# Sixteen instead of eight weight pairs of a second FFN layer by seven block products, with the small elementwise steps placed anew

## The chip, the cores and the metric

The kernel runs on one core of one Trainium2 chip. The metric is the time of one execution on the device in microseconds (us). The engines have short names in the profile: PE is the matrix engine (TensorE), PEld its weight loads, DVE is VectorE, ACT is ScalarE, POOL is GpSimd, and SP (SyncE) issues nearly all DMAs.

## The reference, cut to what matters

```python
xn = _layernorm(x)                                  # x: 2048 x 576
# attention: 32 heads of 18, eight dilated positions (0, 2, .. 14 back) for each token
qkv = xn @ wqkv                                     # 576 x 1728
o = attend(qkv) @ wo                                # 576 x 576
# feed-forward, beside the attention
h = xn @ w1 + b1                                    # 576 x 4608
act = h * tanh(softplus(h))                         # Mish
out = x + o + act @ w2                              # 4608 x 576
```

All values are 32-bit floats. Each matrix product is made of three: both factors are split into a rounded high part and the rest (the low part), and high x high, high x low and low x high are summed in PSUM. Every operand of a product therefore costs elementwise work: a copy to the rounded type on ACT (high) and a subtraction on DVE or POOL (low).

## The kernel before, in words

The 2048 tokens are worked on in two halves of 1024, each split into two blocks b of 512. The hidden width 4608 is cut into 18 pairs q of two 128-wide tiles (j = 0, 1). In each half the plan runs through the QKV products, and then through 18 **quads**, one for a pair q: six parts of the first FFN layer (`m1_part`, L715, already by seven block products) with the second FFN layer's work for the pair before (`add` and `quad`, L1140 to L1270) between them. The second half takes the pairs in the order 1 to 17, then 0 (`Q1`, L33). A last stage multiplies the attention by `wo` (`wo_part`, L1038).

The second FFN layer exists in two forms. In the plain form (`m2_pair` L748, `m2_cols` L861) a quad has four chunks, each of 24 matmuls of 128 x 288 and four DVE additions from PSUM into an accumulator. In the form by **seven products** (`p_item`, L835), which the second half uses for the first `2 * OC` pairs, two pairs are taken together (index e): with the token blocks as rows, the two hidden tiles as the inner index and the two 288-wide column halves as columns, a 2 x 2 block product takes seven products P1 to P7 in place of eight. An item is one product for two pairs: again 24 matmuls of 128 x 288 and four evictions. Two plain quads have 8 chunks, two quads by seven products have 7 items.

For this the left factors S1 to S4 are sums and differences of the activations (`u_sum` L782), and they and the unchanged blocks are split by `u_high` (L792) and `u_low` (L797). The right factors are blocks B11, B21, B22 of w2 and their differences T1 to T4. These are made in half one, when w2 is loaded anyway: `t_sum` (L293), `t_high` (L305), `t_low` (L310), `t_keep` (L315); `keep` (L260) stores the blocks. They go to DRAM and `p_fetch` (L812) brings them back. At the end of that form `p_join` (L855) adds the accumulators of P1, P6 and P7 into those of P2 to P5. One more pair (`a_split`, L804) holds its raw activations and goes the plain way.

Beside this, attention runs as a generator of steps on POOL (products), DVE (reductions) and ACT (exponentials) (`attention`, L512). Its steps are handed to plan slots by weights (`marks`, `rate`, L1481 to L1501). The same 7-product form is used for part of QKV (`z_...`, L383 to L408) and for `wo`; their weight differences are made in half one from quad 9 on (`z_...`, L1376 to L1386) and in half two from quad 11 on (`wo_keep_...`, L1503 to L1514).

The order of instructions on every engine is the order in which the program emits them: for each plan slot first what was put there by `before` (L1144), then the slot's matmuls (L1533 to L1537). Nothing is reordered at run time, so an instruction that waits holds up all behind it on its engine. The lines that place what the change touches:

```python
def before(i, fn):
    plan[max(i, 0)][1].append(fn)
...
for q in range(1, 2 * OC + 1):
    i = spot(0, q, (3,2)[q > 1])
    for (f, name), d in zip(((t_sum, "T3"), (t_sum, "T1"), ...
...
seven = lambda hf, q: hf == 1 and q <= 2 * OC
```

Of the kernel before, what the change touches and what calls it, by code (L numbers as in the profile page):

```python
# [31 lines left out]
OC = 4  # L32
# [5 lines left out]

@with_exitstack
def block_kernel(ctx: ExitStack, tc: tile.TileContext, x, wq, wo, w1, b1, w2, mask, out):  # L40
    nc = tc.nc
    tpn = iter(range(1000))

# [50 lines left out]
    XNB = 5  # L94
# [149 lines left out]
    def make(kind, i):  # L244
        load({"wa": "w1", "wc": "w1", "t0": "w1", "t1": "w1"}.get(kind, kind), i)
        width = home(kind, i)[2]
        if kind == "wa":
            src = loaded["w1", i][0]
        elif kind == "wc":
            src = loaded["w1", i][1][:, 2 * P:5 * P]  # L250
        elif kind in ("t0", "t1"):
            src = sums[i][int(kind[1])]
        else:
            src = loaded[kind, i][:, 0:width]
        t = done[kind, 0, i] = new(kind, 0, i)
        nc.scalar.copy(t[:, 0, :], src)
        low[kind, i] = lambda: nc.vector.tensor_tensor(out=t[:, 1, :], in0=src, in1=t[:, 0, :].bitcast(F32),
                                                       op=ALU.subtract)
# [34 lines left out]
    def t_sum(q, name):  # L293
        eng = nc.vector if name in ("T3",) else nc.gpsimd
        if name in ("T3", "T2"):
            tw[q, name] = sb.tile([P, 5 * P], F32, tag="xn", bufs=XNB, name=f"tw{name}_{q}")[:, 0:D].rearrange(
                "p (c d) -> p c d", c=2)
# [12 lines left out]
    def t_low(q, name):  # L310
        eng = nc.vector
# [60 lines left out]
    zkept, zw, zq, zraw, zhi = {}, {}, {}, {}, {}  # L372
# [10 lines left out]
    def z_load(name, k):  # L383
        t = zraw[name, k] = sb.tile([P, 5 * P], F32, tag="xn", bufs=XNB, name=f"z{name}_{k}")[:, 0:432]
        i = z_unit(name, k)
        nc.sync.dma_start(t, wq[i // 5, i % 5])

    def z_sum(name, k):
        x, y = ZT[name]
        out_ = {"T1": "B12", "T2": "B22", "T4": "B21"}.get(name)  # L390
        if out_ is None:
            zraw[name, k] = sb.tile([P, 5 * P], F32, tag="xn", bufs=XNB, name=f"z{name}_{k}")[:, 0:432]
        else:
            zraw[name, k] = zraw[out_, k]
        nc.gpsimd.tensor_tensor(out=zraw[name, k], in0=zraw[x, k], in1=zraw[y, k], op=ALU.subtract)

    def z_high(name, k):
        hi = zhi[name, k] = sb.tile([P, 5 * P], F32R, tag="xn", bufs=XNB, name=f"zh{name}_{k}")[:, 0:432]
        nc.scalar.copy(hi, zraw[name, k])

    def z_low(name, k):
        t, hi = zraw[name, k], zhi[name, k]
        nc.vector.tensor_tensor(out=t.bitcast(F32R), in0=t, in1=hi.bitcast(F32), op=ALU.subtract)

    def z_keep(name, k):
        d = zkept[name, k] = dram.tile([P, 2 * 432], F32, name=f"kept_{name}_{k}")
        nc.sync.dma_start(d[:, 0:432], zhi[name, k].bitcast(F32))
        nc.sync.dma_start(d[:, 432:864], zraw[name, k])  # L408
# [101 lines left out]
    pend, soon = [], []  # L510

    def attention(hf):  # L512
# [9 lines left out]
        for pair in range(NQ * UQ // PU):  # L522
# [34 lines left out]
            if (hf, pair) == (0, 4):  # L557
                soon.append(lambda: nc.scalar.preload_act_table_set("natural_log_exp_and_others"))
            soon.append(lambda Ls=Ls: nc.scalar.activation(Ls, Ls, AF.Exp, scale=SCALE))
            if (hf, pair) == (0, 4):  # L560
                soon.append(root1)
# [80 lines left out]
    def s_low(hf, c, k):  # L642
        t, hi, lo = stmp[hf, c, k]
        nc.vector.tensor_tensor(out=lo, in0=t, in1=hi.bitcast(F32), op=ALU.subtract)
# [48 lines left out]
    def mish(hf, q, b, j, ph, t=None):  # L693
# [6 lines left out]
        def run():  # L700
# [8 lines left out]
            nc.gpsimd.tensor_tensor(out=a[:, 1, :], in0=t, in1=a[:, 0, :].bitcast(F32), op=ALU.subtract)  # L709
        if q or b != j:  # L710
            pend.append(run)
        else:
            late.append(run)
# [53 lines left out]
    def rslotof(q, x):  # L767
        k = q, int(x[1]) - 1, int(x[2]) - 1
        assert owner[where[k]] == k, (k, owner[where[k]])
# [12 lines left out]
    def u_sum(e, k, qq):  # L782
        name, q = LEFT[ORD[k]], 2 * e + qq
        eng = nc.gpsimd if (name, qq) in (("S1", 1), ("S4", 0)) else nc.vector
# [12 lines left out]
    def u_low(e, k, qq):  # L797
        name, q = LEFT[ORD[k]], 2 * e + qq
        u = unit(e, k, qq)
        eng = nc.gpsimd if (name, qq) in (("S3", 0), ("A22", 0), ("A22", 1), ("A11", 0), ("A11", 1), ("S1", 0), ("A12", 0), ("S2", 0)) else nc.vector  # L800
        eng.tensor_tensor(out=u[:, 1, :], in0=u_src(q, name),  # L801
                          in1=u[:, 0, :].bitcast(F32), op=ALU.subtract)

    def a_split(b, j):  # L804
        q = 2 * OC
        t = rawact[q, b, j]
        assert owner[where[q, b, j]] == (q, b, j) and (q, f"A{b + 1}{j + 1}") in held_
# [47 lines left out]
    def p_join(a, b, pr):  # L855
        nc.gpsimd.tensor_tensor(out=pacc[a, pr], in0=pacc[a, pr], in1=pacc[b, pr], op=ALU.add)  # L856
# [80 lines left out]
    ops, wo_t, wraw, traw = {}, {}, {}, {}  # L937

    wkept, whi = {}, {}

    def wo_keep_high(name, n):
        if name in ("R", "D"):
            src = wraw["R"][:, 0:D] if name == "R" else wraw["D"]
        else:
            src = wo_src(name).rearrange("p k c -> p (k c)")
        w = HC if name == "D" else D
        tag = ("r3", "xn")[n % 2]
        h = sb.tile([P, 2 * 432] if tag == "r3" else [P, 5 * P], F32R, tag=tag, bufs=(1, XNB)[n % 2], name=f"woh_{name}")[:, 0:w]
        whi[name] = h, src
        nc.scalar.copy(h, src)  # L950
        if name == "R":
            d = wraw["D"] = sb.tile([P, 4 * P], F32, tag="tt", bufs=2, name="wo_d")[:, 0:HC]
            nc.gpsimd.tensor_tensor(out=d, in0=src[:, 0:HC], in1=src[:, HC:D], op=ALU.subtract)

    def wo_keep_low(name):
        h, src = whi[name]
        nc.vector.tensor_tensor(out=src.bitcast(F32R), in0=src, in1=h.bitcast(F32), op=ALU.subtract)

    def wo_keep(name):
        h, src = whi[name]  # L960
        w = HC if name == "D" else D
        d = wkept[name] = dram.tile([P, 2, w], F32, name=f"wkept_{name}")
        nc.sync.dma_start(d[:, 0], h.bitcast(F32))
        nc.sync.dma_start(d[:, 1], src)
# [20 lines left out]

    def wo_load(k):
        name = ("B12", "B11", "B21", "B22")[k]
        k0, c0 = (int(name[1]) - 1) * 2 * P, (int(name[2]) - 1) * HC
        wraw[name] = sb.tile([P, 5 * P], F32, tag="raw", bufs=4, name=f"r{name}")[:, 0:D].rearrange(
            "p (k c) -> p k c", k=2)  # L990
        nc.sync.dma_start(wraw[name], wo[k0:k0 + 2 * P, c0:c0 + HC].rearrange("(k p) c -> p k c", p=P))

    def wo_sum(n):
        if n == 0:
            for name in ("T3", "T1", "T2", "T4"):
                traw[name] = sb.tile([P, 5 * P], F32, tag="xn", bufs=XNB, name=f"raw_{name}")[:, 0:D].rearrange(
                    "p (k c) -> p k c", k=2)
        name, x, y = (("T3", "B22", "B12"), ("T1", "B12", "B11"), ("T2", "B22", "T1"), ("T4", "B21", "T2"))[n]
        nc.gpsimd.tensor_tensor(out=traw[name], in0=wo_src(x), in1=wo_src(y), op=ALU.subtract)

    def wo_src(name):
        return (traw if name[0] == "T" else wraw)[name]

    def wo_high(name):
        nc.scalar.copy(wo_t[name][:, 0], wo_src(name))

    def wo_low(name):
        eng = nc.gpsimd if name in ('B21', 'T4') else nc.vector
        eng.tensor_tensor(out=wo_t[name][:, 1], in0=wo_src(name), in1=wo_t[name][:, 0].bitcast(F32),
                                op=ALU.subtract)  # L1010

    def wo_rest(step):
        if step == 0:
            wraw["R"] = raw_load(wo[4 * P:5 * P, :], D, "wo_r")
            return
        r = wraw["R"][:, 0:D].rearrange("p (c d) -> p c d", c=2)
        if step == 1:
            nc.scalar.copy(wo_t["R"][:, 0], r)
            nc.vector.tensor_tensor(out=wo_t["R"][:, 1], in0=r, in1=wo_t["R"][:, 0].bitcast(F32), op=ALU.subtract)
            d = wraw["d"] = sb.tile([P, HC], F32, tag="mn", bufs=5, name="wo_d")  # L1020
            nc.gpsimd.tensor_tensor(out=d, in0=r[:, 0], in1=r[:, 1], op=ALU.subtract)
        else:
            d = wraw["d"]
            nc.scalar.copy(wo_t["D"][:, 0], d)
            nc.vector.tensor_tensor(out=wo_t["D"][:, 1], in0=d, in1=wo_t["D"][:, 0].bitcast(F32), op=ALU.subtract)
# [114 lines left out]
    def add(tag, *fns, alias=None):  # L1140
        at[tag] = at[alias] = len(plan)
        plan.append((list(fns), [], PART[tag[3]] if tag[0] == "m" else US[tag[0]]))

    def before(i, fn):  # L1144
        plan[max(i, 0)][1].append(fn)
# [171 lines left out]

    def bring(kind, i, slot, lead, lag=0):
        before(slot - lead, lambda: load(kind, i))
        before(slot, lambda: make(kind, i))  # L1320
        before(slot + lag, lambda: low[kind, i]())
        before(slot + lag + 3, lambda: keep(kind, i))
# [53 lines left out]
    i = spot(0, 9, 4)  # L1376
    for k in range(2):
        for n, steps in enumerate((
# [205 lines left out]
```

## Time and profile before

| what | value |
| --- | --- |
| median of three runs | 1123.52 us (1123.42 to 1124.13) |
| span of the profiled execution | 1121.6 us |
| instructions in it | 18415 |
| granted TensorE clock, mean of the core | 1.000 |
| PE / PEld busy | 1109.5 / 1023.0 us |
| DVE / POOL / ACT busy | 829.0 / 787.7 / 492.1 us |
| DMA | 271.08 MB, 242 GB/s on average |

The page of the profile tells of one profiled execution from its first to its last instruction; no time of its own stands beside its span. The three runs are timed around the whole execution, and their median is 1.9 us above the span. "Busy" counts instructions from start to end, and for DVE and POOL this takes in what an instruction waits after it has started. The views used below are: the page itself, the list of waits (who waited for whom), the timeline (instructions in order of time, neighbours of one kind merged), busy time by stretches, and groups of instructions by line and shape.

### The profile page before, as it was taken

The numbers are of one execution on the slowest core, as the hardware profiler recorded it, in microseconds if no ns is written. First come the engines' busy times: TensorE is split into PE (matmuls) and PEld (weight loads), VectorE is DVE, ScalarE is ACT, GpSimd is POOL, SyncE is SP. The second block draws the span as 40 slices with busy tenths as digits, with TensorE's granted clock in tenths as the row PEclk, the third lists the DMA queues.
The fourth block names the chain that finished last, engine by engine and source line by source line (L and its number), as shares of the span: only waits on it lengthen the run. The fifth ranks groups of instructions, "written<-read, shape, count | busy, mean of one in ns | idle before, by whom it ended". The sixth has DMA issues, their size and how long they took to land.

```text
span 1121.6 us, 18415 instructions
## 1 busy us (share of the span) xinstructions
PE 1109.5 (99%) x6630; PEld 1023.0 (91%) x6630; DVE 829.0 (74%) x1351; ACT 492.1 (44%) x892; POOL 787.7 (70%) x639
## 2 busy tenths in 40 slices
PE   8999999999999999999999999999999999999998
PEld 7999899999999999899999889999999999999998
DVE  6368788888888888877655456687866677776876
ACT  5544645544554545455233355343433343443332
POOL 2488767767689687676788476665789878668632
PEclk9999999999999999999999999999999999999999
DMA  6899885868767849666596797655655477676463
GB/s 200 283 312 318 290 283 205 289 228 284 261 240 258 282 163 345 222 240 214 191 342 238 231 373 249 241 200 174 227 198 189 168 263 269 215 253 248 157 222 104
DMA packets 147487, 271.08 MB, mean 242 GB/s; under 512 B 30114, under 2 KB 86724, under 8 KB 147396
## 3 DMA queue, kind: packets, MB, share of 16 engines
q1 hardware_dynamic: 147396, 269.91, 69.2%
q8 instruction: 52, 0.85, 0.3%
q14 instruction: 39, 0.32, 0.1%
HBM read 160.39 MB, written 109.48 MB: 241 GB/s over the span
## 4 chain that ended last, share of the span: by engine, by line
PE 89%; DVE 4%; POOL 3%; DMA 2%; issue 1%; ACT 1%; DVEq 0%; POOLq 0%; SPq 0%
PE h L657 28%; PE po L755 19%; PE pq L349 11%; PE po L868 10%; PE po L847 7%; PE h L663 5%; PE o L1056 4%; PE z L447 2%; DMA acc<-in_x 1%; POOL accP L856 1%; DVE u L801 1%; POOL pr L534 0%; DVE accP L871 0%; POOL act L709 0%; DMA z_B<-kept_wq 0%
## 5 line engine op out<-in xcount | busy, mean ns | idle before, releaser
L755 PEld LDWEIGHTS po<-w,act 128*128 128x128 f32 x1728 | 236.4, 188 | 7.5 <-DVE acc L759 1.7
L755 PE MATMUL po<-w,act 128*128 128x288 f32 x1728 | 240.8, 295 | 1.4 <-DVE acc L759 1.2
L534 POOL TENSOR_TENSOR pr<-q,kv 128x576 f32<-128x576 f32 x128 | 195.7, 1553 | 18.7 <-DMA q<-q_d 16.9
L572 POOL TENSOR_TENSOR pv<-L,kv 128x576 f32<-128x576 f32 x128 | 174.3, 1461 | 38.7 <-DVE L L565 20.9
L709 POOL TENSOR_TENSOR act<-c,act 128x512 fp32r<-128x512 f32 x81 | 107.1, 1322 | 128.4 <-ACT act L708 125.5
L759 DVE TENSOR_TENSOR acc<-po,acc 128x288 f32<-128x288 f32 x288 | 120.4, 450 | 31.6 <-PE po L755 30.2
L349 PE MATMUL pq<-wq,xt 128*128 128x432 f32 x672 | 136.2, 361 | 1.8 <-ACT xt L83 1.8
L868 PEld LDWEIGHTS po<-w,act 128*128 128x128 f32 x960 | 131.1, 188 | 3.7 <-DVE accP L871 0.4
L868 PE MATMUL po<-w,act 128*128 128x288 f32 x960 | 133.8, 295 | 0.2
L349 PEld LDWEIGHTS pq<-wq,xt 128*128 128x128 f32 x672 | 125.0, 188 | 8.7 <-ACT xt L83 2.7
L703 ACT ACTIVATE c<-c,b1c 128x512 f32<-128x512 f32 x81 | 58.7, 724 | 132.9 <-DVE c L702 132.6
L657 PE MATMUL h<-xt,t 128*128 128x512 f32 x432 | 110.6, 391 | 0.9 <-DVE c L702 0.8
L657 PE MATMUL h<-S,t 128*128 128x512 f32 x432 | 110.4, 391 | 0.0
L691 ACT COPY c<-h 128x512 f32<-128x512 f32 x81 | 47.4, 586 | 136.5 <-PE h L663 78.3
L578 DVE TENSOR_REDUCE og<-pv 128x144 f32<-128x1152 f32 x64 | 85.9, 1343 | 25.4 <-POOL pv L572 25.4
L657 PE MATMUL h<-xt,wa 128*128 128x512 f32 x432 | 104.0, 390 | 0.0
L657 PEld LDWEIGHTS h<-xt,wa 128*128 128x128 f32 x432 | 80.9, 188 | 16.9
L871 DVE TENSOR_TENSOR accP<-po,accP 128x288 f32<-128x288 f32 x160 | 69.6, 454 | 36.1 <-PE po L868 34.5
L847 PEld LDWEIGHTS po<-pw,u 128*128 128x128 f32 x672 | 92.4, 188 | 2.9 <-DVE u L801 0.5
L847 PE MATMUL po<-pw,u 128*128 128x288 f32 x672 | 94.2, 296 | 0.3 <-DVE u L801 0.3
L539 DVE TENSOR_REDUCE L<-pr 128x64 f32<-128x1152 f32 x64 | 85.8, 1341 | 11.2 <-POOL pr L534 11.1
L657 PEld LDWEIGHTS h<-xt,t 128*128 128x128 f32 x432 | 79.0, 188 | 16.1 <-DVE c L702 1.1
(231 smaller groups left out, 1840.5 us busy)
## 6 DMA issues: line engine op xcount, KB each, us to landing
kv<-kv_d SPq DMA_DIRECT2D x64, 396.0 KB, 5.2
kept_t<-t SPq DMA_DIRECT2D x36, 512.0 KB, 5.3
t<-kept_t SPq DMA_DIRECT2D x36, 512.0 KB, 5.4
rw<-in_w SPq DMA_DIRECT2D x36, 320.0 KB, 4.6
kept_wa<-wa SPq DMA_DIRECT2D x18, 640.0 KB, 3.5
kept_w<-w SPq DMA_DIRECT2D x20, 576.0 KB, 4.8
wa<-kept_wa SPq DMA_DIRECT2D x18, 640.0 KB, 6.1
w<-kept_w SPq DMA_DIRECT2D x20, 576.0 KB, 4.5
```

Of the source, the lines that this page charges most:

```text
L349: nc.tensor.matmul(pq[:, 0:432], XT[:, xi, tok], wt[wi][:, hl, 0:432], start=i == 0, stop=i == len(seq) - 1)
L534: nc.gpsimd.tensor_tensor(out=pr[:, x:x + hh], in0=q[:, j0 + x:j0 + x + hh, None, :].to_broadcast([P, hh, W, CU]), in1=win(kt, 0, CU, j0 + ...
L539: nc.vector.tensor_reduce(L[:, k, j0:j0 + hj].rearrange("p j w h -> p (j w h)"), pr.rearrange("p j w (h d) -> p (j w h) d", h=2), axis=AX, ...
L572: nc.gpsimd.tensor_tensor(out=pr[:, x:x + hj].rearrange("p j d w -> p j w d"), in0=L[:, k, x:x + hj, :, h:h + 1].to_broadcast([P, hj, W, DH]),
L578: nc.vector.tensor_reduce(og[:, :, c0:c0 + DH], pr, axis=AX, op=ALU.add)
L657: nc.tensor.matmul(ph, wt[:, wl, wk * P:(wk + 1) * P], X[:, xs, :], start=first and i == 0, stop=last and i == len(seq) - 1, skip_group_ch ...
L709: nc.gpsimd.tensor_tensor(out=a[:, 1, :], in0=t, in1=a[:, 0, :].bitcast(F32), op=ALU.subtract)
L755: nc.tensor.matmul(po, acts[hf, q, b, j][:, al, tok], done["w2", hf, 2 * q + j][:, wl, c * HC:(c + 1) * HC], start=i == 0, stop=i == 5)
L759: nc.vector.tensor_tensor(out=t, in0=po, in1=t, op=ALU.add)
L847: nc.tensor.matmul(po, units[e, k, qq][:, al, tok], w[:, qq, wl, :], start=i == 0, stop=i == 5)
L868: nc.tensor.matmul(po, acts[hf, q, b, j][:, al, tok], done["w2", hf, 2 * q + j][:, wl, c * HC:(c + 1) * HC], start=i == 0, stop=i == 5)
L871: nc.vector.tensor_tensor(out=t, in0=po, in1=t, op=ALU.add)
```

## The change

- `OC` goes from 4 to 8, so that pairs 1 to 16 (and not 1 to 8) go by seven products in half two. The pair after them, held raw and split by `a_split`, is now the one before the last. The differences of w2 and the block-wise storing follow for pairs 9 to 16.
- The lists `pend` and `soon` and the slots' lists give way to one timeline with six positions for a plan slot. Each elementwise step, load, store and attention step has a key. A table `MOVE` of some 1,600 keys shifts the step by a number of positions (most by less than 20, some by up to 66), and two lists name steps that go to DVE or to POOL instead of their old engine.
- The low half of an activation (`run_low`) is placed apart from the Mish and the high half (`run`).
- The differences and splits of QKV and `wo` weights share one set of functions (`d_load` to `d_keep`), all placed in half one from quad 2 on. `wo`'s leave half two.
- The pool `xn` has 6 buffers instead of 5; T3 and T2 of w2 take buffers of `acc` and `r3`.
- The attention's rates change: 0.6 instead of 0.5 for quads 1 to 8 of half one, and 0.6 instead of 0.8 for quads 9 to 16; in half two 1.0 from quad 2 to quad 16, where 0.8 stood to quad 9 and 1.5 after it.

```diff
-OC = 4
+OC = 8
...
+MOVE = {"0 s_high": -6, "0 s_low": 18, "0 s_step": 3, ... }
+ON_VECTOR = ("act 0_0_12", "act 0_0_13", ... )
+ON_GPSIMD = ("d_low 0 T1", "d_low 1 T1", ... )
...
+    def engine(default, *key):
+        k = " ".join(str(x) for x in key)
+        return nc.vector if k in ON_VECTOR else nc.gpsimd if k in ON_GPSIMD else default
...
-    XNB = 5
+    XNB = 6
...
+    def put(pos, fn, key):
+        pos += MOVE.get(key, 0)
+        assert pos > now[0], key
+        timeline[pos].append(fn)
...
-            nc.gpsimd.tensor_tensor(out=a[:, 1, :], in0=t, in1=a[:, 0, :].bitcast(F32), op=ALU.subtract)
+
+        def run_low():
+            if not seven(hf, q):
+                a = acts[hf, q, b, j]
+                engine(nc.gpsimd, "act", n).tensor_tensor(out=a[:, 1, :], in0=t, in1=a[:, 0, :].bitcast(F32), op=ALU.subtract)
         if q or b != j:
-            pend.append(run)
+            soon(1, 3, run, "mish", n)
+            soon(1, 3, run_low, "act", n)
...
-    def before(i, fn):
-        plan[max(i, 0)][1].append(fn)
+    def before(i, fn, key=None, phase=1):
+        put(max(i, 0) * U + phase, fn, key or name_of(fn))
...
+    i = spot(0, 2, 5)
+    for m, lists in ((0, DIFFS), (1, DIFFS), ("w", DIFFS), ("w", SPLITS)):
...
-             spot(1, 2, 0), spot(1, 2 * OC + 2, 0), spot(1, NP - 1, 0), at["o", 0, 0], at["o", 2, 0]]
-    rate = (1.15, 0.4, 0.5, 0.8, 1.15, 1.3, 1.2, 0.8, 1.5, 0.8, 0)
+             spot(1, 2, 0), spot(1, NP - 1, 0), at["o", 0, 0], at["o", 2, 0]]
+    rate = (1.15, 0.4, 0.6, 0.8, 1.15, 1.3, 1.2, 1.0, 0.8, 0)
```

Counted in the lists, with the keys that no step has left out. To DVE: 29 activation lows of half one (and one of half two), 22 differences of w2, 9 differences of QKV and `wo` weights, 27 `u_low`, 5 `u_sum`, 3 joins. To POOL: 25 lows of loaded weights, 14 `t_low`, 6 lows of QKV and `wo` differences, 4 `s_low`, 17 `u_low`, 18 `u_sum`.

More of the change, by code (lines that the diff above doesn't have):

```diff
@@ L256, in make @@
         nc.scalar.copy(t[:, 0, :], src)
-        low[kind, i] = lambda: nc.vector.tensor_tensor(out=t[:, 1, :], in0=src, in1=t[:, 0, :].bitcast(F32),
+        low[kind, i] = lambda: engine(nc.vector, "low", kind, i).tensor_tensor(out=t[:, 1, :], in0=src, in1=t[:, 0, :].bitcast(F32),
                                                        op=ALU.subtract)
@@ L310, in t_low @@
     def t_low(q, name):
-        eng = nc.vector
+        eng = engine(nc.vector, "t_low", name, q)
         t = tw[q, name]
@@ L397, in z_high @@
[L397 to L408, printed above, removed]
+    PLACE = {"T1": "B11", "T3": "B12", "T2": "B22", "T4": "B21"}
@@ new lines, in d_sum, with d_high @@
+    def d_sum(m, name):
+        if name == "D":
+            r = zraw[m, "R"]
+            x, y, o = r[:, 0:HC], r[:, HC:D], d_tile(m, name)
+        else:
+            x, y = (zraw[m, n] for n in ZT[name])
+            o = zraw[m, PLACE[name]]
+        zraw[m, name] = o
+        engine(nc.gpsimd, "d_sum", m, name).tensor_tensor(out=o, in0=x, in1=y, op=ALU.subtract)
+    def d_high(m, name):
+        hi = zhi[m, name] = d_tile(m, name + "h", F32R)[:, 0:zraw[m, name].shape[1]]
+        nc.scalar.copy(hi, zraw[m, name])
@@ new lines, in d_low, with d_keep @@
+    def d_low(m, name):
+        t, hi = zraw[m, name], zhi[m, name]
+        engine(nc.vector, "d_low", m, name).tensor_tensor(out=t.bitcast(F32R), in0=t, in1=hi.bitcast(F32), op=ALU.subtract)
+    def d_keep(m, name):
+        w = zraw[m, name].shape[1]
+        if m == "w":
+            d = wkept[name] = dram.tile([P, 2, w], F32, name=f"wkept_{name}")
+            nc.sync.dma_start(d[:, 0], zhi[m, name].bitcast(F32))
+            nc.sync.dma_start(d[:, 1], zraw[m, name])
+        else:
+            d = zkept[name, m] = dram.tile([P, 2 * 432], F32, name=f"kept_{name}_{m}")
+            nc.sync.dma_start(d[:, 0:432], zhi[m, name].bitcast(F32))
+            nc.sync.dma_start(d[:, 432:864], zraw[m, name])
@@ L508, in win, with soon, name_of @@
                        ap=[list(base.ap[0]), [CU, jn], [DIL * CU, W], [1, cn]])
-    pend, soon = [], []
+    U = 6
+    now = [0]
+    timeline = []
+    def put(pos, fn, key):
+        pos += MOVE.get(key, 0)
+        assert pos > now[0], key
+        timeline[pos].append(fn)
+    def soon(slots, phase, fn, *key):
+        i = now[0] // U + slots
+        if phase == 3 and i == at["m", 0, 1, 0]:
+            phase = 5
+        put(i * U + phase, fn, " ".join(str(x) for x in key))
+    def name_of(fn):
+        text = lambda x: x.__name__ if callable(x) else str(x)
+        d = [text(x) for x in fn.__defaults__ or ()]
+        return " ".join([x for x in fn.__code__.co_freevars if x not in ("kind", "i", "at", "JB")][:1] + d)
     def attention(hf):
@@ L643, in s_low @@
         t, hi, lo = stmp[hf, c, k]
-        nc.vector.tensor_tensor(out=lo, in0=t, in1=hi.bitcast(F32), op=ALU.subtract)
+        engine(nc.vector, "s_low", hf, c, k).tensor_tensor(out=lo, in0=t, in1=hi.bitcast(F32), op=ALU.subtract)
     acts = {}
@@ L984, in wo_home @@
             wo_t["D"] = t[:, 3, :, 0]
[L986 to L1025, printed above, removed]
     ys = {}
@@ L1315, in block_kernel @@
             add(("o", p, part), lambda p=p, part=part: wo_part(p, part))
+    timeline.extend([] for _ in range((len(plan) + 3) * U))
+    now[0] = -1
+    for i, (fns, _) in enumerate(plan):
+        timeline[i * U + 4].extend(fns)
     def bring(kind, i, slot, lead, lag=0):
[L1319 to L1322, printed above, removed]
+        before(slot - lead, lambda: load(kind, i), f"load {kind} {i}")
+        before(slot, lambda: make(kind, i), f"make {kind} {i}")
+        before(slot + lag, lambda: low[kind, i](), f"low {kind} {i}")
+        before(slot + lag + 3, lambda: keep(kind, i), f"keep {kind} {i}")
     for k in range(5):
@@ L1429, in block_kernel @@
         for c in range(2):
-            before(at["q", 0, 3, 0, 0], lambda c=c, f=f: f(0, c, 3))
+            before(at["q", 0, 3, 0, 0], lambda c=c, f=f: f(0, c, 3), f"{f.__name__} first {c} 3")
     i = at["q", 1, 0, 1, 1]
@@ L1531, in block_kernel @@
             before(at["o", k // 2 - 1, 1], lambda k=k: y_load(k))
-    for i, (fns, bg, _) in enumerate(plan):
-        first, soon[:] = soon[:], []
-        held, pend[:] = pend[:], []
-        for fn in first + bg + (fns + held if i == at["m", 0, 1, 0] else held + fns):
+    for pos, fns in enumerate(timeline):
+        now[0] = pos
+        for fn in fns:
             fn()
```

117 lines of the change are left out of this document (45 added, 72 removed), and 4 rows, old and new, of the table i.

## The prediction

> **What bounds the kernel now.** I read the page first, then who makes PE wait, then PE's timeline around the quads.
>
> ```profile
> span 1121.6 us, 18415 instructions
> PE 1109.5 (99%) x6630; PEld 1023.0 (91%) x6630; DVE 829.0 (74%) x1351; ACT 492.1 (44%) x892; POOL 787.7 (70%) x639
> PEclk9999999999999999999999999999999999999999
> ```
>
> PE is busy in 1109.5 of 1121.6 us, at the full granted clock in all slices. 12.1 us of idle PE are all that better placing alone could win, and part of that is start and end.
>
> ```profile
> ...
> PE o L1056 <- DVE y L1060: 1.3, 2, 0.7
> PE po L755 <- DVE acc L759: 1.2, 1, 1.2
> ...
> PE h L657 <- DVE c L702: 0.8, 1, 0.8
> PE h L657 <- ACT rt L691: 0.7, 1, 0.7
> PE po L847 <- DVE u L801: 0.3, 1, 0.3
> ```
>
> Columns: sum, times, longest. These are the waits of PE behind the start: 4.3 us in six places, 0.72 us each. So time goes only where PE gets less work or new waits. The timeline gives the price of a quad; the rows are the first matmuls of `m1_part` in every second quad, three times by seven products, then twice in the plain form.
>
> ```profile
> 698.54 2.88 PE L657 MATMUL h<-xt,wa 128*128 128x512 f32 x12
> ...
> 743.76 2.88 PE L657 MATMUL h<-xt,wa 128*128 128x512 f32 x12
> ...
> 789.49 2.88 PE L657 MATMUL h<-xt,wa 128*128 128x512 f32 x12
> ...
> 920.27 2.89 PE L657 MATMUL h<-xt,wa 128*128 128x512 f32 x12
> ...
> 968.53 2.89 PE L657 MATMUL h<-xt,wa 128*128 128x512 f32 x12
> ```
>
> Two plain quads take 968.53 - 920.27 = 48.26 us. Two quads by seven products take 45.22 and 45.73 us. The kernel has both forms beside each other, so the main term can be read off directly.
>
> **The change, part by part.**
>
> *Matmuls (removed).* OC from 4 to 8 turns eight more quads, four couples e, into the second form. By the two stretches a couple saves 48.26 - 45.22 = 3.04 or 48.26 - 45.73 = 2.53 us, 2.79 in the mean. The chain of waits gives the same from single pieces:
>
> ```profile
> 703.24 3.24 PE po L847 x24
> ...
> 910.38 3.18 PE po L868 x24
> ```
>
> 8 x 3.18 - 7 x 3.24 = 2.76 us. Four couples: 4 x 2.79 = 11.1 us, between 10.1 and 12.2. I take 11.1, since it holds the small stalls that the form shows already.
>
> *Elementwise work of half two (added).* Groups by line and shape; the last numbers of a row before the second bar are busy us and mean ns.
>
> ```profile
> L709 POOL TENSOR_TENSOR act<-c,act 128x512 fp32r<-128x512 f32 x81 | 107.1, 1322 | 128.4 <-ACT act L708 125.5 <-DMA kv<-kv_d 2.2 <-DMA rw<-in_w 0.8
> L871 DVE TENSOR_TENSOR accP<-po,accP 128x288 f32<-128x288 f32 x160 | 69.6, 454 | 36.1 <-PE po L868 34.5 <-POOL accP L856 0.5 <-issue 0.3
> L853 DVE TENSOR_TENSOR accP<-po,accP 128x288 f32<-128x288 f32 x100 | 40.6, 448 | 7.2 <-PE po L847 6.6 <-POOL accP L833 0.2
> L801 POOL TENSOR_TENSOR u<-ra,u 128x512 fp32r<-128x512 f32 x14 | 18.9, 1354 | 4.7 <-ACT u L795 4.5
> L801 DVE TENSOR_TENSOR u<-rm,u 128x512 fp32r<-128x512 f32 x12 | 11.8, 981 | 3.6 <-ACT u L795 3.6
> L789 POOL TENSOR_TENSOR ra<-ra,rm 128x512 f32<-128x512 f32 x4 | 6.3, 1578 | 0.2
> L789 DVE TENSOR_TENSOR rm<-rt,rm 128x512 f32<-128x512 f32 x6 | 6.1, 1046 | 0.0
> L795 ACT CAST u<-ra 128x512 fp32r<-128x512 f32 x22 | 13.5, 619 | 17.1 <-DVE ra L789 8.4 <-PE po L847 6.9 <-POOL ra L789 1.8
> ```
>
> A couple gains 14 `u_low` (8 x 1.354 on POOL, 6 x 0.981 on DVE) and 8 sums (2 x 1.578, 6 x 1.046), loses 8 activation lows (8 x 1.322), and evicts 28 x 0.448 in place of 32 x 0.454: 10.8 + 5.9 + 3.2 + 6.3 - 10.6 - 2.0 = 13.6 us on DVE and POOL together, 54 for four. ACT gets 6 more copies a couple and 16 in half one, 40 x 0.62 = 25 us on 492: no bound.
>
> *Weight differences (added and moved to half one).*
>
> ```profile
> L303 POOL TENSOR_TENSOR twT<-rw,twT 128x288 f32<-128x288 f32 x16 | 15.9, 997 | 1.3
> L313 DVE TENSOR_TENSOR twT<-twT,twhT 128x576 fp32r<-128x576 f32 x16 | 13.8, 894 | 0.3
> L303 POOL TENSOR_TENSOR twT<-rw 128x288 f32<-128x288 f32 x8 | 9.9, 1235 | 0.0
> L303 DVE TENSOR_TENSOR twT<-rw,rw 128x288 f32<-128x288 f32 x8 | 9.8, 1223 | 0.0
> L957 DVE TENSOR_TENSOR raw_T<-raw_T,woh_T 128x576 fp32r<-128x576 f32 x4 | 5.0, 1238 | 0.0
> L257 DVE TENSOR_TENSOR w<-rw,w 128x576 fp32r<-128x576 f32 x36 | 44.1, 1228 | 5.3 <-ACT w L256 5.3
> ```
>
> Each of eight more quads gets 1.223 + 1.235 + 2 x 0.997 + 2 x 0.894 = 6.2 us, 50 in all. `wo`'s 14 subtractions come over from half two, about 14 x 1.24 = 17 us.
>
> *Does PE cover it?* Busy time by stretches (columns: length, then PE, PEld, DVE, ACT, POOL, clock, DMA share, GB/s):
>
> ```profile
> 145.00:532.00 387.00, 385.75 (x2352) 353.82 (x2351) 326.89 (x521) 194.71 (x317) 284.61 (x240) 1.00 0.71 251
> 338.00:435.00 97.00, 97.00 (x590) 88.93 (x589) 83.28 (x124) 46.17 (x76) 79.93 (x61) 1.00 0.72 256
> 655.00:837.00 182.00, 181.57 (x1090) 165.46 (x1089) 134.96 (x210) 80.12 (x135) 126.40 (x91) 1.00 0.67 233
> 837.00:862.00 25.00, 25.00 (x155) 22.97 (x154) 13.63 (x25) 6.16 (x10) 25.00 (x20) 1.00 0.47 170
> 862.00:1007.00 145.00, 145.00 (x879) 132.79 (x878) 105.47 (x170) 58.20 (x87) 110.11 (x84) 1.00 0.66 229
> 1007.00:1058.00 51.00, 50.57 (x334) 47.31 (x332) 38.91 (x69) 17.58 (x28) 41.07 (x33) 1.00 0.64 227
> ```
>
> Half two (655 to 1058): DVE 293 + POOL 303 = 596 of 806 engine-us, 74%. After: 596 + 54 - 17 = 633 of 2 x 392, 81%. Half one (145 to 532): 327 + 285 = 612 of 774, 79%; after: 612 + 50 + 17 = 679, 88%; attention's rates leave its total there about as it is (8 x 0.5 + 8 x 0.8 against 16 x 0.6, on weights that sum to less). The row 338 to 435 has (83.28 + 79.93) of 194, 84%, with PE busy in 97.00 of 97.00. So half two stays inside what PE is seen to cover, half one goes 4 points beyond.
>
> *Engine changes.* In half one DVE gets 29 activation lows (0.981) and 31 differences (1.223), gives 22 weight lows (1.228; three more lie ahead of the stretch), 14 `t_low` (0.894), 6 lows (1.238). With 8 x (1.223 + 2 x 0.894) and 9 of `wo` x 1.238 this is 326.9 + 24.1 + 11.1 + 28.4 + 37.9 - 27.0 - 12.5 - 7.4 = 381.5 of 387 us, 99%; POOL comes to some 303, 78%. But these durations hold waiting:
>
> ```profile
> 245.19 1.29 POOL L709 TENSOR_TENSOR act<-c,act 128x512 fp32r<-128x512 f32 x1
> ...
> 245.46 1.63 DVE L257 TENSOR_TENSOR w<-rw,w 128x576 fp32r<-128x576 f32 x1
> ...
> 261.82 0.76 DVE L257 TENSOR_TENSOR w<-rw,w 128x576 fp32r<-128x576 f32 x1
> ```
>
> The same DVE subtraction takes 0.76 us or, begun under a POOL instruction, 1.63: it ends at 247.09, 0.61 us behind POOL's end at 246.48. With 0.76/1.228 on all that DVE gains (101.5 us) its need is 343 us, 89%. I take the middle, 94%: full, but with deadlines that the slots' lead can meet. In-order queues make the cost: behind a subtraction that waits stand the evictions, and behind these PE, which needs free PSUM.
>
> *Removed waits.* The 4.3 us of PE waits may partly go with the new places, or others come: between -4.3 and, in half one, the rival below. I take 0.
>
> *Stores and fetches.* Eight quads of half one store 7 x 288 KB instead of 2 x 576, by the program: 864 KB more in 24.2 us, 36 GB/s on 256, a DMA share of about 0.82 after 0.72. A store waits on SP for its low half, with the loads of later quads behind it:
>
> ```profile
> SPq L275 <- DVE w L257: 48.9, 14, 6.2
> ```
>
> The longest such wait, 6.2 us, is a quarter of a quad, and loads go out five slots (about half a quad) ahead. Nothing at this cover; without it a late load would stop PE for some us in a quad. In half two four couples fetch 28 blocks of 576 KB where eight plain quads fetched 16: 12 more transfers in some 180 us at a share of 0.66, hidden.
>
> *Joins.* They move from 820 to 866 us to the last quad and the chunks behind it: no change but for the rival below.
>
> *Sum.* 1121.6 - 11.1 = 1110.5 us of span. The runs' median is 1.9 us above the span: **1112.4 us**.
>
> **The rivals.**
>
> *DVE late in half one.* For it: 89 to 99% of DVE. Against it: the row at 84% of both engines shows no wait at all. A wait of 0.72 us in every second of 16 quads is 5.8 us: 1118 us.
>
> *Slower: DVE and POOL read SBUF by turns.* For it: the rows at 245 and 261 us. Count all POOL time as holding and each DVE subtraction with its 0.76: now, in 338 to 435, 79.9 + (24 weight lows + 8 of QKV) x 0.76 = 104 of 97 us, 1.07, and PE doesn't wait. So the count is too high by at least that. After the change half one has about 303 + 179 x 0.76 = 439 of 387, 1.13 (74 weight lows, 29 activation lows, 31 differences, 16 T3, 18 `t_low`, 11 others). If 1.07 were the ceiling, half one would need 439/1.07 = 410 us: 23 us more than now, 1135 us. It decides from 1.07 on. Against it: many are 288 to 512 wide and shorter than 0.76, and moving a low from POOL (1.322) to DVE shortens the sum. The Trainium skill's page "SBUF — State Buffer", section "Who interferes with whom", says that a DVE instruction with two SBUF inputs and a POOL instruction that reads SBUF exclude each other for the whole instruction, so that moving work between the two frees less than it seems. By that rule the two rows agree (0.61 us behind POOL's end), and the time would be this rival's.
>
> *The last quads.*
>
> ```profile
> L856 POOL TENSOR_TENSOR accP<-accP,accP 128x576 f32<-128x576 f32 x14 | 20.5, 1485 | 1.2 <-DVE accP L853 1.2
> ```
>
> 11 of 14 joins stay on POOL, 11 x 1.485 = 16.3 us in a stretch where it has 41.07 of 51: 57 of 51 if no attention leaves it. At most 6 us late: 1118.
>
> *Placing also wins.* All six waits go and the couples reach 3.04: 1123.5 - 12.2 - 4.3 = 1107 us.
>
> That the change does not do what it says is excluded by the count of items that the program asserts (L1401).
>
> **How the numbers follow.** Forecast (1109 to 1115) 0.62; DVE late (1115 to 1122) 0.17; by turns 0.07; last quads 0.07; placing wins 0.07. I call 0.2% (2.2 us) what a measurement can tell: faster is below 1121.3, slower above 1125.8. Faster: 0.62 + 0.15 + 0.07 + 0.07 = 0.91, less 0.01 for what I don't see: 0.90. Same 0.04 (the end of DVE late and the beginning of by turns), slower 0.06. The range 1108.5 to 1120 leaves out about 0.04 below and 0.10 above.
>
> **What would show it.** Right: quads 9 to 15 of half two at 45.2 to 45.7 us a couple, PE busy near 1098 us, L868 with 8 x 96 = 768 fewer matmuls and L847 with 672 more, quads of half one still 24.1 us apart. Wrong: half one's quads further apart with PE waiting for DVE's evictions (L759) or additions (L702), DVE subtractions well above 1.2 us in the mean, or PE waiting at the end for accumulators that POOL joins.

## The result and the profile after

| | before | after |
| --- | --- | --- |
| median, four runs each on one chip | 1123.47 us | 1108.51 us (1107.54 to 1110.24) |
| ratio, 95% interval | | 0.9868 (0.9854 to 0.9882) |
| span of the profiled execution | 1121.6 us | 1106.9 us |

The change gains 15.0 us where 11.1 were forecast (1112.4 us, range 1108.5 to 1120). Of its four executions, two had a mean granted clock of 0.998 and spans of 1106.9 and 1107.6 us, two 1.000 and 1106.4 and 1105.8; the profile is of the first. The page of the changed kernel:

```profile
span 1106.9 us, 18216 instructions
PE 1097.6 (99%) x6534; PEld 1012.0 (91%) x6534; DVE 864.5 (78%) x1419; ACT 509.6 (46%) x933; POOL 818.3 (74%) x659
```

96 matmuls are gone. PE's busy time falls by 11.9 us and its idle time by 2.8 (12.1 to 9.3): together the 14.7 us of the span. Who makes PE wait (sum, times, longest), all there is:

```profile
PE z L477 <- DVE zqs L490: 1.8, 1, 1.8
PE warm L76 <- POOL ident masks.py:199: 1.3, 1, 1.3
PE pq L359 <- ACT xt L92: 1.2, 2, 0.6
PE h L705 <- ACT rt L739: 0.7, 1, 0.7
PE o L1041 <- DVE y L1045: 0.6, 1, 0.6
PE pq L359 <- POOL wq L1158: 0.2, 1, 0.2
```

The waits for the second FFN layer (`po`) and for `c` are gone; one in the z stage (QKV of half two by seven products, between the halves) is new. The couples of half two in the timeline, every second quad:

```profile
698.72 2.88 PE L705 MATMUL h<-xt,wa 128*128 128x512 f32 x12
...
743.75 2.93 PE L705 MATMUL h<-xt,wa 128*128 128x512 f32 x12
...
788.82 2.93 PE L705 MATMUL h<-xt,wa 128*128 128x512 f32 x12
...
834.29 2.93 PE L705 MATMUL h<-xt,wa 128*128 128x512 f32 x12
...
879.36 2.93 PE L705 MATMUL h<-xt,wa 128*128 128x512 f32 x12
...
924.44 2.93 PE L705 MATMUL h<-xt,wa 128*128 128x512 f32 x12
...
969.68 2.93 PE L705 MATMUL h<-xt,wa 128*128 128x512 f32 x12
```

All six steps are nearly alike now, 45.03 to 45.47 us: (969.68 - 698.72) / 6 = 45.16 us in the mean. Busy time by stretches (length, then PE, PEld, DVE, ACT, POOL, clock, DMA share, GB/s): half one, its middle, half two.

```profile
145.00:532.00 387.00, 387.00 (x2361) 355.02 (x2360) 354.62 (x577) 209.31 (x342) 298.71 (x254) 1.00 0.84 291
338.00:435.00 97.00, 97.00 (x590) 88.92 (x589) 85.47 (x144) 54.35 (x91) 67.67 (x56) 1.00 0.84 297
655.00:1007.00 352.00, 351.89 (x2105) 320.56 (x2105) 282.15 (x438) 150.61 (x249) 273.56 (x197) 1.00 0.65 235
```

In half one PE doesn't stop at all, beside a DVE that is busy in 354.62 of 387 us.

### The profile page after: what moved, and what is told of

It is laid out like the page before. It is cut to its first block, busy times and chain, and to the rows that moved or that the text cites. A ratio compares the mean times of both kernels' runs of the same rounds, so it can differ in the third digit from the quotient of the medians.

```text
span 1106.9 us, 18216 instructions
## 1 busy us (share of the span) xinstructions
PE 1097.6 (99%) x6534; PEld 1012.0 (91%) x6534; DVE 864.5 (78%) x1419; ACT 509.6 (46%) x933; POOL 818.3 (74%) x659
## 4 chain that ended last, share of the span: by engine, by line
PE 91%; POOL 3%; DVE 2%; DMA 1%; ACT 1%; issue 1%; POOLq 0%; ACTq 0%
PE h L705 31%; PE po L808 21%; PE po L900 16%; PE pq L359 8%; PE h L711 6%; PE o L1041 4%; PE z L477 2%; PE po L921 2%; POOL s L656 1%; POOL pr L582 1%; DVE og L626 0%; POOL pv L620 0%; DMA q_d<-qs 0%; DMA o_d<-og 0%; POOL s_u L656 0%
## 5 line engine op out<-in xcount | busy, mean ns | idle before, releaser
L808 PEld LDWEIGHTS po<-w,act 128*128 128x128 f32 x1728 | 236.5, 188 | 5.6
L808 PE MATMUL po<-w,act 128*128 128x288 f32 x1728 | 240.6, 295 | 0.0
L900 PEld LDWEIGHTS po<-pw,u 128*128 128x128 f32 x1344 | 184.0, 188 | 5.1 <-DVE u L854 0.5
L900 PE MATMUL po<-pw,u 128*128 128x288 f32 x1344 | 187.1, 295 | 0.1
L906 DVE TENSOR_TENSOR accP<-po,accP 128x288 f32<-128x288 f32 x212 | 89.0, 450 | 33.0 <-PE po L900 28.8
L705 PEld LDWEIGHTS h<-S,t 128*128 128x128 f32 x432 | 78.1, 188 | 13.0
L761 POOL TENSOR_TENSOR act<-c,act 128x512 fp32r<-128x512 f32 x38 | 53.2, 1402 | 33.0 <-ACT act L756 33.0
L751 ACT ACTIVATE c<-c,b1c 128x512 f32<-128x512 f32 x57 | 41.3, 724 | 68.1 <-DVE c L750 68.0
L739 ACT COPY c<-h 128x512 f32<-128x512 f32 x57 | 33.3, 584 | 54.7 <-PE h L705 29.7
L705 PE MATMUL h<-S,wc 128*128 128x512 f32 x216 | 55.7, 393 | 0.7 <-ACT rt L739 0.7
```

What stands on the lines that cost most here:

```text
L705: nc.tensor.matmul(ph, wt[:, wl, wk * P:(wk + 1) * P], X[:, xs, :], start=first and i == 0, stop=last and i == len(seq) - 1, skip_group_ch ...
L761: engine(nc.gpsimd, "act", n).tensor_tensor(out=a[:, 1, :], in0=t, in1=a[:, 0, :].bitcast(F32), op=ALU.subtract)
L808: nc.tensor.matmul(po, acts[hf, q, b, j][:, al, tok], done["w2", hf, 2 * q + j][:, wl, c * HC:(c + 1) * HC], start=i == 0, stop=i == 5)
L900: nc.tensor.matmul(po, units[e, k, qq][:, al, tok], w[:, qq, wl, :], start=i == 0, stop=i == 5)
L906: nc.vector.tensor_tensor(out=t, in0=po, in1=t, op=ALU.add)
```

## The experiments

All are compared with the kernel before on the same chip (1123.5 to 1123.8 us).

**Is PE still the bound?** `matmuls_back` issues the 24 matmuls of P3 twice in the four new couples. It gives back the 96 matmuls and nothing else.

```diff
-                for i in range(6):
+                for i in 2 * [*range(6)] if e >= 4 and name == "P3" else range(6):
```

> The changed kernel with the 96 matmuls put back that the four new couples save: product P3 of each of them is computed twice into the same PSUM bank, the second time over the first. All elementwise work, its engines and its places stay. Theory, PE is still the bound: 96 x 0.129 to 0.1325 us = 12.4 to 12.7 us more, 1121 us. Rival, DVE and POOL bound the new quads too, so that PE has slack in them: less than 8 us more.

Measured: 1122.69 us, 0.999 (0.9981 to 0.9999).

```profile
span 1122.5 us, 18408 instructions
PE 1110.5 (99%) x6630; PEld 1023.6 (91%) x6630; DVE 862.2 (77%) x1419; ACT 509.6 (45%) x933; POOL 816.5 (73%) x659
```

The 96 matmuls cost 14.2 us in the time, a little above the 12.4 to 12.7 expected, and 12.9 in PE's busy time, 134 ns each. With the same count of matmuls both kernels take the same time to 0.1% (1.1 us). So nearly all of the gain over the kernel before is the matmuls' own. PE's idle time is back at 12.0 us here (1122.5 - 1110.5), in a profiled execution that is 1.6 us above the median.

**Would the matmuls pay without the places?** Four kernels: without shifts and lists (`neither`), the same with `OC = 4` (`neither_oc4`), without the shifts alone (`no_move`), without the lists alone (`no_lists`).

```diff
-MOVE = {"0 s_high": -6, "0 s_low": 18, ... }
+MOVE = {}
-ON_VECTOR = ("act 0_0_12", "act 0_0_13", ... )
-ON_GPSIMD = ("d_low 0 T1", "d_low 1 T1", ... )
+ON_VECTOR = ()
+ON_GPSIMD = ()
```

> The table of shifts and both engine lists are emptied; everything else is as in the changed kernel (16 pairs by seven products). Theory, the matmuls taken away pay by themselves and the placing only removes some waits of PE: PE busy near 1098 us, time 1111 to 1117 us. Rival, only the placing makes the 16 pairs pay: PE busy again near 1098 us but over 15 us of new waits of PE, most of them for DVE in half one, time 1123 us or more.

> As the kernel with neither shifts nor lists, and OC back at 4, so 8 pairs by seven products. Theory: four couples of quads more in the plain form, 10.1 to 12.2 us above the kernel with neither shifts nor lists at OC 8, and PE busy 12 us more. Rival (placing decides, matmuls are eaten): within 4 us of it, since with less elementwise work its waits fall as its matmuls rise.

> The shifts are emptied, the two engine lists stay. Theory: the lists change which engine does a step but not when, so between the changed kernel and the one with neither: 1109 to 1117 us. Rival (the lists were made for the shifted places and load DVE in half one to 94% and more): slower than with neither, with PE waits for DVE in half one.

> The engine lists are emptied, the shifts stay. Theory: DVE and POOL of half one come to about 362 and 318 of 387 us instead of 355 and 299, still covered; 1109 to 1115 us. Rival (DVE and POOL read SBUF by turns, so that POOL's longer hold decides): PE waits in half one, 1116 us or more.

| | us | ratio to before |
| --- | --- | --- |
| neither, 16 pairs | 1183.18 | 1.0538 (1.0508 to 1.0568) |
| neither, 8 pairs | 1166.89 | 1.0384 (1.0369 to 1.0400) |
| no shifts | 1184.88 | 1.0542 (1.0512 to 1.0571) |
| no lists | 1166.54 | 1.0388 (1.0372 to 1.0403) |

My theory falls: without the places sixteen pairs are 16.3 us slower than eight, though they have 96 matmuls less. By the starts of PE's rows they lose 16.1 us in half one (448.8 against 432.7) and 5.4 in the z stage, and win only 4.8 in half two. Shifts and lists belong together: the shifts alone win 16.6 of the 74.7 us between `neither` and the changed kernel, the lists alone nothing that can be told (1184.88 against 1183.18). (In these kernels the differences of `wo` and QKV stay in half one, and steps without a shift stand where the new timeline puts them. The old hand-made order with sixteen pairs was not tried.) `no_lists` came out where the rival of engines that take turns had it, 1116 us or more, but doesn't show that cause: its half one is 44.5 us longer than the changed kernel's, with only 12 us more of busy time on DVE and POOL together (374 + 337 against 376 + 324). PE's waits in `neither`:

```profile
PE h L705 <- DVE c L750: 21.6, 9, 5.3
PE h L705 <- DVE rt L750: 11.3, 9, 1.9
PE po L900 <- DVE accP L906: 4.3, 6, 1.6
PE z L477 <- DVE zqs L490: 4.1, 1, 4.1
```

Its half one, over about the matmuls that the changed kernel does from 145 to 532 us:

```profile
145.00:564.00 419.00, 399.29 (x2355) 362.62 (x2354) 358.77 (x554) 209.10 (x341) 319.84 (x270) 0.97 0.76 268
```

The stretch is 32 us longer: PE stands idle for 20 of them, and at the lower clock (0.97) the same matmuls take 12 more. DVE is busy in 359 us and POOL in 320, 4 and 21 more than in the changed kernel, but DVE is also idle in 60 us, where it was in 32. So it isn't only the fill of an engine that decides. The longest wait in the timeline of `neither` shows what else does; the rows are of PE, DVE, POOL and ACT (start, us, and in brackets the idle time before it and who ended it):

```profile
349.79 2.92 PE L705 MATMUL h<-xt,t 128*128 128x512 f32 x6 [5.30 <-DVE c L750]
...
347.89 1.24 DVE L323 TENSOR_TENSOR twT<-twT,twhT 128x576 fp32r<-128x576 f32 x1 [2.74 <-ACT twhT L318]
349.05 0.68 DVE L750 TENSOR_TENSOR c<-h,c 128x512 f32<-128x512 f32 x1
...
343.10 3.30 POOL L582 TENSOR_TENSOR pr<-q,kv 128x576 f32<-128x576 f32 x2
346.37 0.78 POOL L313 TENSOR_TENSOR twT<-rw,twT 128x288 f32<-128x288 f32 x1
347.19 0.67 ACT L318 CAST twhT<-twT 128x576 fp32r<-128x576 f32 x1 [4.42 <-POOL twT L313]
```

Read it backwards. PE waits for an addition (L750) that frees PSUM. That addition stands on DVE behind the low half of a weight difference (L323), which waits 2.74 us for its high half on ACT, which waits for the difference on POOL, which stands behind 3.30 us of attention. None of these weights is wanted before half two. In eight waits of half one, 19.5 us, the addition stands behind such a low half; in five of them, 18.0 us, DVE itself stands idle for the high half or the difference.

**Is it this queue, or capacity?** `t2_later` is `neither` with the high half, the low half and the store of T2 one slot (six positions) later in quads 1 to 16, so that the low half finds its input ready. It does the same work.

```diff
-MOVE = {}
+MOVE = {"t_high T2 1": 6, "t_low T2 1": 6, "t_keep T2 1": 6, ... "t_keep T2 16": 6}
```

> The kernel with eight sixteenth pairs by seven products and without shifts and lists (1183.2 us), with one thing moved: in quads 1 to 16 of half one the high, low and store of the weight difference T2 stand one slot later. Theory (head of the line: the low of a difference waits on DVE for ACT and POOL, and DVE's evictions stand behind it, 19.5 us of PE's waits in eight places): most of these waits go and the kernel takes 1158 to 1168 us. Rival (DVE and POOL together lack the time in half one, so another instruction is late instead): 1180 us or more.

Measured: 1167.13 us, 1.0385 (1.0366 to 1.0403), 16.1 us less than `neither`: for these the queue.

```profile
PE h L705 <- DVE rt L750: 11.2, 9, 1.9
PE h L705 <- DVE c L750: 8.1, 8, 2.3
```

The waits for `c` fall from 21.6 to 8.1 us and the longest from 5.3 to 2.3; those for `rt`, which belong to half two, stay. By the starts of PE's rows half one takes 430.8 us, 18.0 less than in `neither`, although DVE and POOL are busy for longer in it (388 and 354 us after 384 and 348). The changed kernel takes 412.9. So this one place is worth half of what `neither` loses in half one. No run takes apart the other half, nor the 35.0 us that it loses in half two (448.3 against 413.3).

**How much lead is left in half one?** `dve_2` computes the low halves of w2 in half one once more on DVE (two instructions per quad), `dve_6` those of w1 too (six per quad). `before_dve_2` does to the kernel before what `dve_2` does to the changed one, and `pool_2` puts the two on POOL. The second one writes the same values again.

```diff
-        low[kind, i] = lambda: engine(nc.vector, "low", kind, i).tensor_tensor(out=t[:, 1, :], ...
+        def lows():
+            again = kind == "w2"
+            for eng in [engine(nc.vector, "low", kind, i)] + again * [nc.vector]:
+                eng.tensor_tensor(out=t[:, 1, :], in0=src, in1=t[:, 0, :].bitcast(F32), op=ALU.subtract)
+        low[kind, i] = lows
```

> The changed kernel with the low halves of the w2 tiles of half one computed twice on DVE right behind each other, two subtractions of 128x576 more in each quad of half one. Theory, DVE in half one (354.6 of 387 us busy) has some 30 us left and the places have little lead: 16 x 2 x 0.75 to 1.0 us = 24 to 32 us more of DVE just fit in, but deadlines slip; 3 to 12 us more. Rival, DVE and POOL reading by turns is already the limit: all of it shows, 24 us or more. Other rival, the lead is ample: less than 2 us.

> As the run with two more subtractions in each quad, but with all six weight lows of a quad of half one (w1's four and w2's two) computed twice. Theory, past the capacity of DVE: 16 x 6 x 0.7 to 0.9 us = 67 to 86 us of DVE where some 30 are left, so 35 to 60 us more. Rival, by turns: what counts is the hold of SBUF, all of it shows, 65 us or more.

> The kernel before, with two more DVE subtractions in every quad of half one (the low halves of w2, computed once more), 24 to 32 us of DVE time as in the changed kernel with the same addition, where all of it came out, 32 us. Theory (the change spent slack that half one had; DVE stood at 327 of 387 us and now at 355): the kernel before takes up most of it, 0 to 15 us slower than without, 1124 to 1139 us. Rival (its order had no lead either; a queue in order lets any added instruction through to PE): 24 us or more, 1148 us and above.

> The changed kernel, with the same two low halves of w2 per quad of half one computed once more on POOL in place of DVE, about 2 x 18 POOL instructions of 1.3 us. Theory (the two engines read SBUF by turns, so POOL time blocks DVE as DVE time does): as much as on DVE, 30 to 45 us slower, 1138 to 1153 us. Rival (only DVE's queue is full; POOL has 88 of 387 us idle in half one): under 10 us, 1110 to 1118 us.

| | us | ratio to before | against the same kernel without the addition |
| --- | --- | --- | --- |
| dve_2 | 1140.53 | 1.0158 (1.0142 to 1.0174) | +32.0 |
| dve_6 | 1208.36 | 1.0771 (1.0734 to 1.0807) | +99.9 |
| before_dve_2 | 1133.95 | 1.0088 (1.0071 to 1.0105) | +10.2 |
| pool_2 | 1142.77 | 1.0166 (1.0151 to 1.0181) | +34.3 |

DVE's busy time grows by 32.2 us in `dve_2` (864.5 to 896.7) and by 42.5 in `before_dve_2` (829.0 to 871.5). The kernel before takes up three quarters of the addition; the time of the changed one grows by as much as was added. That the two agree so well is partly chance: of 31.2 us more of span, 23.4 are PE's idle time (32.7 after 9.3) and 7.8 the same matmuls at a lower clock (0.994 in the mean). In `before_dve_2` these are 6.0 and 6.5 us. The pair isn't quite equal: eight of the 36 lows of w2 lie on POOL after the change, and the repeated one on DVE then waits for POOL's. DVE's waits in half one of `dve_2`:

```profile
DVE w L269 <- POOL w L269: 14.0, 4, 6.2
```

Even if these 14.0 us came through whole, 18 of 32 are left against 10 of 42. So my expectation that the new order has slack left was wrong, and the one behind `before_dve_2`, that the change spent lead which half one had, holds. `dve_6` is much the same: 98 us more of DVE (864.5 to 962.9) for 99.9 us, of which 68 are PE's idle time and 32 the lower clock (0.977).

`pool_2` lands in the range of the theory of taking turns, as `dve_2` and `dve_6` did in theirs, but its trace tells more. The loss is made by the end of half one. Two groups of DVE there that have two inputs in SBUF (mean ns behind the comma; the lines stand three lower than in the changed kernel), and below them the same groups of the changed kernel from 145 to 532 us:

```profile
L326 DVE TENSOR_TENSOR twT<-twT,twhT 128x576 fp32r<-128x576 f32 x17 | 20.5, 1209 | 0.5 <-ACT twhT L321 0.3
L269 DVE TENSOR_TENSOR wa<-rw,wa 128x640 fp32r<-128x640 f32 x13 | 18.4, 1414 | 1.1 <-ACT wa L265 1.1
...
L323 DVE TENSOR_TENSOR twT<-twT,twhT 128x576 fp32r<-128x576 f32 x17 | 17.2, 1015 | 0.4 <-ACT twhT L318 0.4
L266 DVE TENSOR_TENSOR wa<-rw,wa 128x640 fp32r<-128x640 f32 x13 | 13.1, 1008 | 0.5 <-ACT wa L265 0.5
```

But over all of DVE this lengthening is 11.2 us (864.5 to 875.7), a third of the loss, while DVE stands idle 20 us more: in 421 us of half one it waits 6.4 us for attention's products, 3.6 for differences and 6.6 for transfers around them, with PSUM evictions behind each, at once or a few instructions later. The lengths fit DVE and POOL taking turns; by these sums most of the price came through the queues. The Trainium skill's page "SBUF — State Buffer", section "Who interferes with whom", has the turns as its rule; the longer rows agree with it, but no run here separates it fully from the waits.

**The new wait in the z stage.** In the changed kernel PE, DVE and POOL there:

```profile
606.72 1.69 PE L477 MATMUL z<-z_B,S 128*128 128x432 f32 x6 [1.82 <-DVE zqs L490]
...
603.37 1.35 DVE L587 TENSOR_REDUCE L<-pr 128x64 f32<-128x1152 f32 x1 [0.86 <-POOL pr L582]
...
606.00 0.45 DVE L490 TENSOR_TENSOR zkv<-z,zkv 128x288 f32<-128x288 f32 x1
...
593.69 1.30 POOL L656 TENSOR_TENSOR s<-s,s_u 128x512 f32<-128x512 f32 x1
594.93 8.40 POOL L582 TENSOR_TENSOR pr<-q,kv 128x576 f32<-128x576 f32 x6
```

The evictions of z (L490) come behind attention's last reduction and softmax, these wait for POOL's products, and these began behind sums of x (L656). Two kernels try to remove it by shifts: `late_softmax` puts the softmax 11 positions later, behind the evictions; `sums_later` puts the sums of x and their two rounding steps behind the products.

```diff
-"att 67": 6
+"att 67": 17
```

> The changed kernel with one attention step (the reduction of the last products of half one's last pair and its softmax up to the exponential, on DVE) moved behind the evictions of the QKV item in front of which it stands. Theory: the 1.8 us wait of PE there goes, and with it the lower granted clock of the microseconds after it; 3 us faster than the changed kernel, about 1105.5 us. Rival: the next step is late instead, and the time stays at 1108.5 us.

Measured: 1117.48 us, 0.9958 (0.9938 to 0.9978), 9 us slower than the changed kernel. With the shift the exponential comes behind three attention products that take its output, so these are computed from the values before it and the kernel stands here for its time alone.

```profile
PE z L477 <- ACT zqs L486: 8.3, 1, 8.3
```

DVE's evictions are in time now, but the exponential waits on ACT for those products, and ACT's evictions of z stand behind it.

```diff
-"s_step 1 3": -7, "s_high 1 3": -15, "s_low 1 3": -2
+"s_step 1 3": 19, "s_high 1 3": 5, "s_low 1 3": 6
```

> The changed kernel, with the last three rounding steps of x in the z stage (the sum on POOL and the two that follow it on DVE and ACT) put three to four slots later, so that POOL does attention's last products ahead of them and the softmax ends about 4 us earlier. Theory (the one new wait of the z stage, 1.8 us, comes from POOL's queue, and the lowered clock behind it costs as much again): the wait goes and the kernel takes about 1105.5 us, 3 us less than the changed kernel. Rival (the order only moves the lateness to another step): 1108.5 us or more, with another wait of PE in the same stage.

Measured: 1114.82 us, 0.9918 (0.9903 to 0.9933), 6.3 us slower than the changed kernel. PE's wait:

```profile
PE z L477 <- POOL xt L692: 4.4, 1, 4.4
```

and POOL in its timeline:

```profile
608.46 7.06 POOL L620 TENSOR_TENSOR pv<-L,kv 128x576 f32<-128x576 f32 x6 [3.01 <-issue]
615.42 1.26 POOL L692 TENSOR_TENSOR xt<-s,xt 128x512 fp32r<-128x512 f32 x1
```

The wait behind the softmax is gone here too, but the low half of x (L692) now stands on POOL behind 7.06 us of attention's second products, and the matmuls need it. Both times the lateness only moved. No version was found that beats the changed kernel.

## Why the prediction was right, and where it was not

*What bounds the kernel.* Right: with 96 matmuls put back the time is that of before.

*Matmuls, 11.1 us.* Right in kind, mis-sized. Four couples give 4 x (48.26 - 45.16) = 12.4 us, just above the bounds of 10.1 to 12.2. The prediction kept the small stalls that the old couples showed (45.73 us for one of them); the new ones are all near the shortest.

*Removed waits, "I take 0".* Too small for three stages and blind to a fourth. The stages of the two profiled executions, by the starts of PE's rows, in us:

| stage | before | after | difference |
| --- | --- | --- | --- |
| to the first FFN product | 100.60 | 100.04 | -0.56 |
| half one, to the first transposes for half two (`tt`) | 415.34 | 412.93 | -2.41 |
| QKV of half two, plain part | 73.56 | 73.55 | -0.01 |
| z stage, to the first FFN product of half two | 38.01 | 41.48 | +3.47 |
| half two, to the first product by `wo` (`o`) | 427.72 | 413.31 | -14.41 |
| the rest | 66.37 | 65.59 | -0.78 |

Half two wins 2.0 us beyond the 12.4 of its couples and half one 2.4, where two waits of PE (1.2 and 0.8 us) are gone; the z stage takes 3.5 back. All but the matmuls makes -2.3 us, together the 14.7 us of the span. So the time comes nearest to the rival "placing also wins" (1107 us), which had a chance of 0.07, and the range held it by 0.01 us (1108.5 against 1108.51): that is luck. How much of the 2.3 us is the places' own stays open. `matmuls_back`, in the same places, is 1.1 us faster than the kernel before in the median; in its profiled execution half one wins 1.3 us, half two 0.9 (426.80 us) and the z stage loses 4.2.

*Elementwise work.* The times were close. DVE in half one: 343 to 382 forecast, 354.62 measured; POOL 303, now 298.71; half two 81% of both engines, now (282.15 + 273.56) / 704 = 79% from 655 to 1007 us; half one 88%, now 653 / 774 = 84%, since most rows became shorter:

```profile
L266 DVE TENSOR_TENSOR w<-rw,w 128x576 fp32r<-128x576 f32 x28 | 27.7, 990 | 0.5 <-ACT w L265 0.5
```

That was 1228 ns before, in the group that the sum used; DVE's differences, 1223 ns there, are now at 704 to 924. The `t` group did not fall (1175 ns, now 1245).

*The step that held without support* is "full, but with deadlines that the slots' lead can meet". It was drawn from the totals, as if PE's cover followed from the fill of DVE and POOL. In the changed kernel the deadlines were met: PE doesn't wait in half one, and "DVE late" (1115 to 1122 us) did not come. But the runs show that the totals don't decide it: `t2_later` has DVE and POOL busy for longer in half one than `neither` and is 16.1 us faster. Lead is a property of the order, instruction by instruction; here the shifts and lists made it, and by `dve_2` they left little to spare. The forecast was right because the places were good, which the totals could not tell. With no placing worked out, the chance of slower (0.06) was too low for what the trace had shown.

*By turns, 1135 us.* It did not come: PE waits nowhere in half one. The count of 1.13 did not decide.

*Stores and fetches, joins.* Right: a DMA share of 0.84 (0.82 forecast) without a wait of PE, and in the last quads only 0.6 us for `y`.

*What would show it.* Couples of 45.2 us, PE busy 1097.6 us (near 1098) and half one without a gap came as named. What was not named is the z stage: from quad 17 of half one to quad 2 of half two the way grew from 149.28 to 152.77 us.

## What to carry to other kernels

When a change takes work from the bounding engine and gives it to others, the busy shares of these say only whether it can fit. Whether it does hung here, for the 16 us that a run could isolate, on who stood in front of the PSUM evictions in a queue. Look, for each added instruction, at what it waits for and what is queued behind it, and give steps whose result is wanted late their place behind those that PE waits for. Test the lead that is left by adding a few instructions: if most of their time shows, the next change needs new places as well.

## What the hardware showed beside this

A short wait of PE can cost more than itself. Around the wait of 1.82 us in the changed kernel:

```profile
604.00:606.00 2.00, 0.90 (x5) 0.51 (x3) 1.90 (x4) 0.00 (x0) 0.59 (x1) 1.00 1.01 404
606.00:608.00 2.00, 1.28 (x6) 1.20 (x7) 1.93 (x8) 0.42 (x1) 0.00 (x0) 0.94 1.02 385
608.00:610.00 2.00, 2.00 (x7) 1.83 (x6) 0.42 (x1) 0.58 (x2) 1.35 (x2) 0.50 0.25 93
610.00:612.00 2.00, 2.00 (x9) 1.87 (x8) 0.92 (x1) 0.58 (x2) 2.00 (x2) 0.71 0.00 1
612.00:614.00 2.00, 2.00 (x12) 1.94 (x11) 0.96 (x2) 0.00 (x0) 2.00 (x3) 1.00 0.00 0
```

The granted clock falls to 0.50 after PE has begun again. The shortfall is (0.06 + 0.50 + 0.29) x 2 = 1.7 us at full clock, or 3.4 us at half. With the wait that is 3.5 us, the whole loss of the z stage. The Trainium skill's page "TensorE: Matmul & The Clock Gate", section "What's actually happening", states a half clock after at least one idle window of about 3.4 us, and the full clock after a busy one of about that length. The half clock and its 3.4 us agree; but PE had not been idle for 3.4 us, only for 1.82, and the measurement decides here.

It doesn't follow every short wait. In `neither` the granted clock fell to about half after all five waits of PE of 2.87 us and more, and after only two (1.75 and 1.90 us) of the twelve between 1.1 and 2.1 us. The two executions of the changed kernel with a mean clock of 1.000 can't have had the 1.7 us either.

In `neither` PE has the same 6534 matmuls as in the changed kernel, but is busy 1121.6 us instead of 1097.6, at a mean clock of 0.984 instead of 0.998: some 1182.5 x 0.014 = 17 of these 24 us are lost to the lower clock.
